# A fused attention and mixture-of-experts kernel: three early blocks of one expert, three of the second, then a fourth of each, in an order that is computed anew

## The chip, the core and the metric

The kernel runs on one core of a Trainium2 chip. Its metric is the device time of one execution in microseconds (us). The engines are PE (TensorE: matmuls, with its weight loads listed apart as PEld), DVE (VectorE), ACT (ScalarE), POOL (GpSimd) and SP (SyncE, which issues most DMAs). Each engine works through a queue of its own in the order in which the program was written, and waits at the head of that queue for whatever the next instruction needs.

## The reference

A causal attention with a sliding window, then a mixture of eight experts of which each row uses two:

```python
B, H, S, D = 8, 8, 576, 64
scores = q @ k.T / sqrt(D) + slopes[h] * -|i - j|      # kept where 0 <= i - j < 128
attn   = exp(scores - max); attn /= attn.sum() + 1e-9
x      = (attn @ v) laid out as 4608 rows x 512
logits = x @ w_gate + log1p(exp(x @ w_noise)) * noise   # 8 experts
top2   = the two largest of each row; weights = softmax over the two
for e in range(8):                                      # w1 512 x 1024, w2 1024 x 512
    out[rows of e] += weight * (relu(x[rows of e] @ w1[e]) @ w2[e])
```

## The kernel before

**The stages.** The attention comes as 32 pairs of heads (8 batches of 4 pairs), and each pair makes nine score blocks along the sequence, 288 in all. For each block PE computes the scores (L518), DVE adds the bias and finds the maxima (L524, two instructions a block), ACT takes the exponentials (L532), PE transposes them (L539), ACT or DVE copies them out of the accumulator bank, and PE multiplies by the values (L553). When a batch is done, `rows` divides by the denominators, writes the rows to memory and computes the gate; `route` then picks the two experts of each row, and gives each its place in the lists of the experts (`slots`).

**The experts.** A matrix is kept as two half-precision parts, high and low, and each product is three matmuls. `weight` loads one eighth (a *step*, 512 KB) of an expert's two matrices into one of 24 tiles `held`, and takes its absolute maxima (`wam`): on ACT as two activations that write into `junk` (L1147), on DVE as one reduction (L1143). When all eight steps of an expert have theirs, `powers_of_weights` makes a power of two from them, and `split` writes the high halves (a copy with a scale, L287 on ACT and L289 on DVE) and the low halves (L1185 on DVE, L1182 and the line behind it on POOL) over the raw weights. `tokens` gathers a block's rows by an indirect DMA (L1218); `fit` scales and splits them (the last part is L1256), and a transposing DMA (L1264) brings them into `ax` or `bx`. `mm1` (L1273) makes a step of the hidden layer; `middle` applies the relu (high part on ACT, L1301, or on DVE; low part always on DVE, L1324, into `ahl` or `bhl`); `mm2` (L1333) multiplies by the second matrix.

**Two waves.** The first wave has eight small blocks, four of each of the first two experts: 256, 256, 256 and 192 rows. The fourth of an expert, say, is written 0.3 for expert 0. The rows of such a block are taken from the lists as they stand after 2, 4, 6 and 7 of the 8 batches (`CUTS`; the ids that belong to them come from L1008), so that the first wave runs while the attention still goes on. `SEQUENCE` is the order of these blocks. The second wave has the rest: one block for each of the first two experts and three for each of the others. Between the waves `overflow` computes on one partition a table of the rows that an expert has beyond its capacity (L1549 to L1574, in the tiles `spared`).

**What sets the order.** No loop order is written out. While the program is built, `Order` plays the whole run through with a duration for each operation. Each step is a strand that yields its operations with a rank, and an engine of the model takes the one with the lowest rank among those that are ready; what is taken is written into the program at that place. A strand that yields an operation of several instructions (a lambda with a list) has them in one piece. `either(...)` offers an operation to ACT and to DVE, each with its own duration and rank offset, and the first to take it keeps it. The numbers at the top of the program are ranks and offsets: `WEIGHTS` and `HOLD` for when an expert's steps are loaded, `GATE` for the rows of a batch, `FFN0` and `FFN1` for the early blocks, `BIG` and `PARTS` for the maxima and the halves of the later experts' weights, `LATE` for the second engine of an `either`. For POOL, the model also blocks DVE for a fixed time beside three of its operations (`slows`).

In the time after, lines 5 to 6 lower in number mean the same operations (L1324 before is L1319 after, L1143 and L1147 are L1141 and L1145).

Of the kernel before, what the change touches and what calls it, by code (L numbers as in the profile page):

```python
# [15 lines left out]
OP = mybir.AluOpType  # L16
AX = mybir.AxisListType
# [5 lines left out]
NQ = 5  # L23
# [19 lines left out]
ZERO = 714.8  # L43
LOAD = 296.4
VALUES = 533.9
GATE = (-2.7, -33.5)
ROUTE = 0
SCATTER = (-245.2, -812.9, 94.5)
FFN0, FFN1 = 207.0, 403.8
WEIGHTS = ((-24.5, 112.1), (505.6, 7.5))  # L50
SEQUENCE = ((0, 0), (0, 1), (1, 0), (1, 1), (0, 2), (1, 2), (0, 3), (1, 3))
TOKENS = -211.8
STAGE = (130.6, -162.3, -306.6, -45.6, -45.9, -85.0, 118.1, -29.9)
MIDDLE = 410.3
RESULT = -460.1
WEIGHTS_LATE = 152.7
SOON = 370.9
LISTED = (-405.9, 168.6)
BIG, PARTS = -57.2, 468.7
TIGHT = (1, 5, 7)  # L60
LATE = (-344.6, -113.3, -185.1, 116.9, -276.1, 92.1, -240.2, -276.5, 251.3, -261.2, 47.5, 142.3, 39.7, 106.3)
# [4 lines left out]
REST = 5.6  # L66
PACE = (8.9, 10.6)
HOLD = (-83.6, 40.7)
AHEAD = -25.9
GATHER_LAG, SCATTER_LAG, LISTED_LAG, TURN_LAG = 4.4, 5.0, 3.0, 4.0  # L70
STAY, TURN = -100.0, 0.13
# [16 lines left out]
class Op:  # L88


    def __init__(self, on, emit, join=True, shape=0, slows=0.0):
        self.slows = slows
        self.on, self.emit, self.join, self.taken = on, emit, join, False
        self.shape, self.leaves = shape if isinstance(shape, tuple) else (shape, shape)
# [16 lines left out]
class Order:  # L111
# [136 lines left out]
def attention_moe(ctx: ExitStack, tc: tile.TileContext, qk_, v, w_gate, w_noise, noise, w12,  # L248
# [410 lines left out]
    def rows(b, t):  # L659
# [5 lines left out]
        def turned():  # L665
            for e in range(2):
                for h in range(2):
                    from_ = (h + e) % 2 * 64
                    nc.vector.tensor_scalar(den[e * 64:e * 64 + 64, 0:NQ - e, h:H:2], dens[b][from_:from_ + 64, e:NS:2], 1e-9, None,
                                            op0=OP.add)  # L670
# [111 lines left out]
    def route(b):  # L782
# [160 lines left out]
        else:  # L943
            yield Op((("POOL", 1.55, rank), ("DVE", 0.8, rank + LATE[10])), lambda g: tables(engine[g], 2), slows=0.4)
# [185 lines left out]
    def weight(e, f, t, rank):  # L1130
# [44 lines left out]
    def split(e, f, z, t, parts, rank, both):  # L1175
# [11 lines left out]
        if e < EARLY:  # L1187
            yield Op((("POOL", 2.85, rank), ("DVE", 0.66, rank + WEIGHTS_LATE)), low, slows=0.6)
# [195 lines left out]
    def last_downs(blk, rank):  # L1384
# [15 lines left out]
        for z, on in enumerate(("ACT", "DVE")):  # L1400
# [138 lines left out]
    def overflow():  # L1539
# [20 lines left out]
        def compare():  # L1560
            V.tensor_tensor(ge[:, 0], jt[:, :, None].to_broadcast(shape), cnt[:, 3:4].to_broadcast(shape), op=OP.is_ge)
            V.tensor_mul(ge[:, 1], ge[:, 0], cnt[:, 1:2].to_broadcast(shape))

        def rows():
            V.tensor_reduce(red, ge, axis=AX.X, op=OP.add)
# [4 lines left out]
            V.tensor_mul(ge[:, 0], ge[:, 0], capv[:, None, :].to_broadcast(shape))  # L1570
            V.tensor_reduce(jt, ge[:, 0], axis=AX.X, op=OP.add)
# [157 lines left out]
```

## Time and profile before

| what | before |
|---|---|
| device time, median of 3 runs | 1053.86 us (1053.57 to 1054.55) |
| the profiled execution | 1055.3 us, span of the trace 1053.5 us |
| mean granted clock of TensorE | 0.993 |
| PE busy | 1014.3 us, 96% of the span |
| DVE busy | 633.3 us, 60% |
| ACT busy | 495.2 us, 47% |
| POOL busy | 346.4 us, 33% |
| DMA, mean over the span | 137 GB/s |

An engine's busy share is a mean over stages that are limited by different things. DVE and ACT are nine tenths busy in the first slices, while the attention runs, and at two to four tenths from the middle on, where PE multiplies by the experts' weights without a break. So the table says which engine is fullest over the whole span, and the stretches have to be looked at one by one. The idle time of PE (the span less 1014.3 us) is 39.2 us.

### The profile page before, as it was taken

The numbers are of one execution on the slowest core, as the hardware profiler recorded it, in microseconds if no ns is written. First come the engines' busy times: TensorE is split into PE (matmuls) and PEld (weight loads), VectorE is DVE, ScalarE is ACT, GpSimd is POOL, SyncE is SP. The second block draws the span as 40 slices with busy tenths as digits, with TensorE's granted clock in tenths as the row PEclk, the third lists the DMA queues.
The fourth block names the chain that finished last, engine by engine and source line by source line (L and its number), as shares of the span: only waits on it lengthen the run. The fifth ranks groups of instructions, "written<-read, shape, count | busy, mean of one in ns | idle before, by whom it ended". The sixth has DMA issues, their size and how long they took to land.

```text
span 1053.5 us, 23716 instructions
## 1 busy us (share of the span) xinstructions
PE 1014.3 (96%) x8942; PEld 639.7 (61%) x8942; DVE 633.3 (60%) x2264; ACT 495.2 (47%) x1402; POOL 346.4 (33%) x458
## 2 busy tenths in 40 slices
PE   7989798999999899999999999999999999999997
PEld 4756666776676579754565457545744664564455
DVE  8998998978787982254559544744494364332111
ACT  8998887766422552231346333632353343332211
POOL 1476963334233431330333232312332320421102
PEclk9999999999999999999999999999999999999999
DMA  9868796635258882385765576519563752653113
GB/s 339 329 233 284 249 305 202 184 96 122 35 108 247 172 105 38 87 190 171 103 144 107 112 151 126 124 40 173 122 135 50 150 82 51 122 68 52 17 24 50
DMA packets 130340, 144.79 MB, mean 137 GB/s; under 512 B 90400, under 2 KB 91504, under 8 KB 130224
## 3 DMA queue, kind: packets, MB, share of 16 engines
q1 hardware_dynamic: 112704, 103.92, 36.1%
q0 software_dynamic: 17520, 39.34, 21.8%
q8 instruction: 71, 1.16, 0.5%
q14 instruction: 45, 0.37, 0.1%
HBM read 82.89 MB, written 40.91 MB: 118 GB/s over the span
## 4 chain that ended last, share of the span: by engine, by line
PE 81%; DVE 12%; ACT 4%; issue 2%; POOL 1%; DMA 0%; DVEq 0%; POOLq 0%; ACTq 0%
PE bank L1273 34%; PE bank L1333 28%; PE bank L1338 6%; PE bank L553 4%; PE bank L518 3%; PE bank L539 3%; DVE p L524 3%; ACT p L532 2%; DVE held L1185 1%; DVE x L704 1%; PE bank L724 1%; ACT pT L287 1%; DVE xt L1256 1%; PE bank L1446 1%; PE bank L701 1%
## 5 line engine op out<-in xcount | busy, mean ns | idle before, releaser
L1273 PEld LDWEIGHTS <-held 128*128 128x128 f16 x2424 | 234.7, 98 | 124.5 <-issue 0.6
L1273 PE MATMUL bank<-bx,held 128*128 128x512 f16 (+7 forms) x1752 | 300.6, 324 | 0.0
L1324 DVE SCALAR_TENSOR_TENSOR bhl<-bank,bhh 128x384 f16<-128x384 f32 (+6 forms) x152 | 84.6, 557 | 281.2 <-ACT bhh L1301 281.0
L1468 POOL DMA_INDIRECT out_dram<-yo,ix x62 | 99.4, 1603 | 426.6 <-ACT yo L287 366.8
L1301 ACT ACTIVATE bhh<-bank 128x512 f16<-128x512 f32 (+6 forms) x134 | 65.4, 488 | 325.9 <-PE bank L1273 317.2
L1333 PE MATMUL bank<-held,bhh 128*128 128x512 f16 x696 | 207.0, 379 | 0.0
L1333 PE MATMUL bank<-held,bhl 128*128 128x512 f16 x348 | 131.9, 379 | 0.0
L532 ACT ACTIVATE p<-p,nm 128x192 f32<-128x192 f32 (+2 forms) x288 | 121.9, 428 | 14.0 <-DVE nm L524 13.6
L1333 PEld LDWEIGHTS <-bhh 128*128 128x128 f16 x768 | 75.2, 98 | 80.7
L1218 POOL DMA_INDIRECT xg<-xs_dram,ix x62 | 69.2, 1116 | 51.9 <-issue 16.6
L524 DVE CUSTOM_DVE_ANT_0 p<-bank,bias 128x192 f32<-128x192 f32 (+2 forms) x288 | 79.6, 328 | 9.5 <-PE bank L518 6.6
L518 PE MATMUL bank<-qk 64*64 64x192 f32 (+2 forms) x1152 | 67.0, 328 | 12.2 <-DVE nm L524 8.5
L1273 PE MATMUL bank<-ax,held 128*128 128x256 f16 (+1 forms) x672 | 77.0, 268 | 0.0
L539 PE MATMUL bank<-ident,p 128*128 128x128 f32 x416 | 67.5, 285 | 9.2 <-ACT pT L287 2.2
L287 ACT ACTIVATE held<-held,wsc 128x512 f16<-128x512 f32 x96 | 65.7, 716 | 17.6 <-DVE held L1185 16.2
L1333 PEld LDWEIGHTS <-bhl 128*128 128x128 f16 x384 | 37.6, 98 | 45.5 <-DVE bhl L1324 0.5
L539 PEld LDWEIGHTS bank<-ident,p 128*128 128x128 f32 x416 | 44.7, 141 | 31.9 <-ACT p L532 10.5
L1143 DVE TENSOR_REDUCE wam<-held 128x2 f32<-128x1024 f32 x53 | 63.7, 1210 | 0.3 <-DMA held<-in_w_dram 0.3
L1185 DVE SCALAR_TENSOR_TENSOR held<-held,wsc,held 128x512 f16<-128x512 f32 x88 | 63.2, 756 | 0.0
L553 PE MATMUL bank<-pT,vraw 64*64 64x64 f32 (+1 forms) x2048 | 61.3, 227 | 0.4 <-DVE x L704 0.3
L553 PEld LDWEIGHTS bank<-pT,vraw 64*64 64x64 f32 (+1 forms) x2048 | 55.1, 138 | 8.8 <-issue 3.5
L287 ACT ACTIVATE xt<-xg,fit 128x512 f16<-128x512 f32 (+5 forms) x60 | 43.0, 718 | 32.6 <-DVE fit L1232 30.9
(254 smaller groups left out, 1499.3 us busy)
## 6 DMA issues: line engine op xcount, KB each, us to landing
held<-in_w_dram SPq DMA_DIRECT2D x60, 512.0 KB
qk<-in_qk_dram SPq DMA_DIRECT2D x31, 576.0 KB
vraw<-in_v_dram SPq DMA_DIRECT2D x16, 640.0 KB
out_dram<-xg SPq DMA_DIRECT2D x10, 1024.0 KB
xs_dram<-x SPq DMA_DIRECT2D x32, 256.0 KB
spare<-in_w_dram SPq DMA_DIRECT2D x4, 512.0 KB
xs_dram<-x SPq DMA_DIRECT2D x8, 128.0 KB
xs_dram<-xg SPq DMA_DIRECT2D x1, 1024.0 KB
```

The costliest lines, as they stand in the source:

```text
L287: nc.scalar.activation(o, i, AF.Copy, **kw)
L518: nc.tensor.matmul(s[j % 2][half:half + 64, o:o + c], qk[rows, j * 64:j * 64 + 64], qk[rows, k1 - c:k1], start=True, stop=True)
L524: nc.vector.tensor_tensor_reduce(out=p[:, place(j):place(j) + c], in0=s[z][:, o:o + c], in1=bias4[:, g, z, 192 - c:192], scale=-0.125, sca ...
L532: nc.scalar.activation(pv, pv, AF.Exp, bias=nm[:, z:z + 1], scale=-1.0, accum_out=den[:, j, g:g + 1])
L539: nc.tensor.transpose(t[:, z * 128:z * 128 + 128], p[:, a * 128:a * 128 + 128], ident)
L553: nc.tensor.matmul(o[half, j // 2 * SUB:j // 2 * SUB + SUB], t[rows, block, hh:hh + D], pt[rows, slot, from_:from_ + 64], start=first_, st ...
L1185: nc.vector.scalar_tensor_tensor(lo, t, sc, hi, op0=OP.mult, op1=OP.subtract)
L1218: yield pool(1.04, rank, lambda: nc.gpsimd.indirect_dma_start(out=xg[0:r], out_offset=None, in_=xs[0:blk.rows], in_offset=bass.IndirectOff ...
L1273: nc.tensor.matmul(t[:, 0:blk.n], wp[:, c], blk.x[:, x + c, 0:blk.n], start=c == 0 and z == 0, stop=c == 3 and z == 2)
L1324: yield dve(0.07 + c * 0.00104, rank - MIDDLE, lambda: nc.vector.scalar_tensor_tensor(hl[:, 0:c], t[:, 0:c], 0.0, hh[:, 0:c], op0=OP.max, ...
L1333: nc.tensor.matmul(blk.y[j][0:r], h[:, cs], wp, start=f == 0 and m == 0, stop=f == 7 and m == 2)
L1468: ins = nc.gpsimd.indirect_dma_start(out=out, out_offset=bass.IndirectOffsetOnAxis(ap=blk.ix[0:r, j:j + 1], axis=0), in_=t[0:r], in_offset ...
```

## The change

All edits are in the program that computes the order and in the steps that it places; the matmuls are the same.

- The early blocks come as 0.0, 0.1, 0.2, 1.0, 1.1, 1.2, 0.3, 1.3, where they alternated from the third on.
- The second expert's eight steps are loaded later, by `WEIGHTS` and `HOLD`.
- The sums of the denominators in `rows` go to POOL (to DVE for the last batch), and the reciprocal becomes an operation of its own on DVE.
- The maxima of all experts' weights may be taken by ACT or DVE, where those of the later six were DVE's alone. The low halves of the third expert may be made on POOL, as those of the first two.
- The table of the overflow is twelve operations in the queue, in place of two that had 2 and 10 instructions.
- The last block's second half of a result is copied by ACT, where DVE did it.
- `slows` goes: the model no longer blocks DVE beside POOL.
- All ranks and offsets have new values, and the order is made anew with them.

```diff
-WEIGHTS = ((-24.5, 112.1), (505.6, 7.5))
-SEQUENCE = ((0, 0), (0, 1), (1, 0), (1, 1), (0, 2), (1, 2), (0, 3), (1, 3))
+WEIGHTS = ((63.8, 81.5), (510.7, 23.6))
+SEQUENCE = ((0, 0), (0, 1), (0, 2), (1, 0), (1, 1), (1, 2), (0, 3), (1, 3))
...
-BIG, PARTS = -57.2, 468.7
+BIG, PARTS = 30.4, 41.2
...
-HOLD = (-83.6, 40.7)
+HOLD = (-77.6, 178.2)
...
-    def __init__(self, on, emit, join=True, shape=0, slows=0.0):
-        self.slows = slows
+    def __init__(self, on, emit, join=True, shape=0):
...
-        elif e == "POOL" and what.slows:
-            self.busy["DVE"] = max(self.busy["DVE"], self.now) + what.slows
-            self.at(self.busy["DVE"], lambda: self.dispatch("DVE"))
...
-        def turned():
+        on = nc.vector if b == B - 1 else nc.gpsimd
+
+        def collected():
             for e in range(2):
                 for h in range(2):
...
-                    nc.vector.tensor_scalar(den[...], dens[b][...], 1e-9, None, op0=OP.add)
-            nc.vector.reciprocal(den, den)
-        yield dve(1.3, rank, turned)
+                    on.tensor_scalar(den[...], dens[b][...], 1e-9, None, op0=OP.add)
+        yield (dve if b == B - 1 else pool)(1.0, rank, collected)
+        yield dve(0.36, rank, lambda: nc.vector.reciprocal(den, den))
...
-        if e < EARLY:
-            yield either(1.35, 1.13, rank, LATE[12], largest)
-        else:
-            yield dve(1.13, rank + BIG, lambda: largest("DVE"))
+        yield either(1.6, 1.13, rank + (BIG if e >= EARLY else 0), LATE[12 if e < EARLY else 14], largest)
...
-        if e < EARLY:
-            yield Op((("POOL", 2.85, rank), ("DVE", 0.66, rank + WEIGHTS_LATE)), low, slows=0.6)
+        if e <= EARLY:
+            yield Op((("POOL", 2.85, rank), ("DVE", 0.66, rank + WEIGHTS_LATE)), low)
...
-        for z, on in enumerate(("ACT", "DVE")):
+        for z, on in enumerate(("ACT", "ACT")):
...
-        yield dve(1.5, 1110, compare)
-        yield dve(2.2, 1120, rows)
+        for z, (us, emit) in enumerate(steps_):      # the same twelve instructions
+            yield dve(us, 1130 + 2 * z, emit)
```

Three places show what this does to the queues. The first is DVE's queue at the overflow's table, while the early blocks run. `spared` are the tiles of the table, `ahl` the low parts of the hidden layer, `wam` the maxima of the third expert's raw weights in `held16` and its followers. Before:

```order
L1568 CAST bias4_135<-spared_5082 1x80
L1569 TENSOR_TENSOR spared_5082<-iota8_142,spared_5082 1x640
L1570 TENSOR_TENSOR spared_5082<-spared_5082,capv_197 1x640
L1571 TENSOR_REDUCE spared_5082<-spared_5082 1x80
L1572 SCALAR_TENSOR_TENSOR spared_5082<-spared_5082 1x80
L1573 SCALAR_TENSOR_TENSOR spared_5082<-spared_5082 1x80
L1574 TENSOR_SCALAR bias4_135<-spared_5082 1x80
L1324 SCALAR_TENSOR_TENSOR ahl1_212<-bank5_71,ahh1_209 128x256
L1143 TENSOR_REDUCE wam_189<-held16_5065 128x2
L1324 SCALAR_TENSOR_TENSOR ahl2_213<-bank0_66,ahh2_210 128x256
L1143 TENSOR_REDUCE wam_189<-held17_5066 128x2
L1143 TENSOR_REDUCE wam_189<-held18_5067 128x2
```

After, from a little earlier in the table on:

```order
L1319 SCALAR_TENSOR_TENSOR ahl2_213<-bank0_66,ahh2_210 128x256
L1559 TENSOR_SCALAR spared_5158<-spared_5158 1x80
L1560 TENSOR_TENSOR spared_5158<-spared_5158 1x80
L1561 CAST bias4_135<-spared_5158 1x80
L1562 TENSOR_TENSOR spared_5158<-iota8_142,spared_5158 1x640
L1319 SCALAR_TENSOR_TENSOR ahl0_211<-bank1_67,ahh0_208 128x256
L1563 TENSOR_TENSOR spared_5158<-spared_5158,capv_197 1x640
L1564 TENSOR_REDUCE spared_5158<-spared_5158 1x80
L1319 SCALAR_TENSOR_TENSOR ahl1_212<-bank5_71,ahh1_209 128x256
L1565 SCALAR_TENSOR_TENSOR spared_5158<-spared_5158 1x80
L1566 SCALAR_TENSOR_TENSOR spared_5158<-spared_5158 1x80
L1567 TENSOR_SCALAR bias4_135<-spared_5158 1x80
```

The operations of the table no longer stand in one row: three of L1319 (L1324 before) stand among them, and no `wam` of the third expert follows.

The second place is SP's queue at the loads of the second expert's eight steps (`held8` to `held15` out of `in_w_dram`). Before, they stand among the first loads of the attention (`qk`, `vraw`, and the noise `noi`), ahead of all rows of the first batch:

```order
L415 DMA noi_141<-in_noise_dram 128x320
L1135 DMA held8_121<-in_w_dram 128x1024
L1135 DMA held9_122<-in_w_dram 128x1024
L1135 DMA held10_123<-in_w_dram 128x1024
L1135 DMA held11_124<-in_w_dram 128x1024
L1135 DMA held12_125<-in_w_dram 128x1024
L471 DMA vraw1_83<-in_v_dram 128x1280
L1135 DMA held13_126<-in_w_dram 128x1024
L457 DMA qk1_79<-in_qk_dram 128x1152
L1135 DMA held14_127<-in_w_dram 128x1024
L1135 DMA held15_128<-in_w_dram 128x1024
L418 DMA slots_dram<-xg2_133 128x352
```

After, they stand between rows of the third batch (`x0` to `x3`, written to `xs_dram`) and the store of a gate (`gd`):

```order
L707 DMA xs_dram<-x3_109 128x512
L1133 DMA held8_121<-in_w_dram 128x1024
L467 DMA vraw0_82<-in_v_dram 128x1280
L1133 DMA held9_122<-in_w_dram 128x1024
L1133 DMA held10_123<-in_w_dram 128x1024
L1133 DMA held11_124<-in_w_dram 128x1024
L1133 DMA held12_125<-in_w_dram 128x1024
L1133 DMA held13_126<-in_w_dram 128x1024
L1133 DMA held14_127<-in_w_dram 128x1024
L1133 DMA held15_128<-in_w_dram 128x1024
L453 DMA qk3_81<-in_qk_dram 128x1152
L976 DMA xs_dram<-gd_178 128x4x8
```

The eight loads have moved by some 75 places in SP's queue; the same instructions, the same sizes.

The third place is ACT's queue where the second wave begins: `ahh` are the high parts of the last early block, `bhh` those of the first block of the second wave. Before:

```order
L1301 ACTIVATE ahh1_209<-bank5_71 128x192
L1301 ACTIVATE ahh2_210<-bank0_66 128x192
L1301 ACTIVATE ahh0_208<-bank1_67 128x192
L287 ACTIVATE yt0_5083<-bank7_73 128x192
L287 ACTIVATE yt1_5084<-bank3_69 128x192
L287 ACTIVATE yt2_5085<-bank6_72 128x192
L287 ACTIVATE yt3_5086<-bank4_70 128x192
L287 ACTIVATE yo1_205<-bank2_68,gw4_202 128x512
L287 ACTIVATE yo2_5073<-bank2_68,gw4_202 64x512
L1301 ACTIVATE bhh1_5060<-bank0_66 128x256
L1301 ACTIVATE bhh2_5061<-bank1_67 128x256
L1301 ACTIVATE bhh0_5059<-bank5_71 128x256
```

After:

```order
L1296 ACTIVATE ahh0_208<-bank1_67 128x192
L1296 ACTIVATE ahh1_209<-bank5_71 128x192
L1296 ACTIVATE ahh2_210<-bank0_66 128x192
L1145 ACTIVATE junk_188,wam_189<-held16_5141 128x512 x2
L1145 ACTIVATE junk_188,wam_189<-held17_5142 128x512 x2
L1145 ACTIVATE junk_188,wam_189<-held18_5143 128x512 x2
L1145 ACTIVATE junk_188,wam_189<-held19_5144 128x512 x2
L1145 ACTIVATE junk_188,wam_189<-held20_5145 128x512 x2
L1145 ACTIVATE junk_188,wam_189<-held21_5146 128x512 x2
L1296 ACTIVATE bhh2_5137<-bank1_67 128x256
L1296 ACTIVATE bhh0_5135<-bank5_71 128x256
L1145 ACTIVATE junk_188,wam_189<-held23_5148 128x512 x2
```

Between the last early block and the second wave's first relus on ACT stand six pairs of maxima of the third expert's weights, and a seventh pair two relus later; before there were results of an early block (`yt`, `yo`) and no maxima.

More of the change, by code (lines that the diff above doesn't have):

```diff
@@ L42 @@
 LISTS = ((0, EARLY, DONE[-1], (CAP - DONE[-1] + 127) // 128), (EARLY, E, 0, (CAP + 127) // 128))
[L43 to L46, printed above, removed]
+ZERO = 781.9
+LOAD = 234.3
+VALUES = 544.1
+GATE = (-40.1, -141.2)
 ROUTE = 0
-SCATTER = (-245.2, -812.9, 94.5)
-FFN0, FFN1 = 207.0, 403.8
-WEIGHTS = ((-24.5, 112.1), (505.6, 7.5))
-SEQUENCE = ((0, 0), (0, 1), (1, 0), (1, 1), (0, 2), (1, 2), (0, 3), (1, 3))
[L52 to L58, printed above, removed]
-BIG, PARTS = -57.2, 468.7
+SCATTER = (15.2, -920.1, 412.5)
+FFN0, FFN1 = 185.5, 400.5
+WEIGHTS = ((63.8, 81.5), (510.7, 23.6))
+SEQUENCE = ((0, 0), (0, 1), (0, 2), (1, 0), (1, 1), (1, 2), (0, 3), (1, 3))
+TOKENS = -212.1
+STAGE = (310.1, -61.0, -339.5, -54.3, 18.9, -292.4, 181.0, 131.1)
+MIDDLE = 85.6
+RESULT = -852.8
+WEIGHTS_LATE = 159.2
+SOON = 274.1
+LISTED = (-393.8, 515.9)
+BIG, PARTS = 30.4, 41.2
 TIGHT = (1, 5, 7)
-LATE = (-344.6, -113.3, -185.1, 116.9, -276.1, 92.1, -240.2, -276.5, 251.3, -261.2, 47.5, 142.3, 39.7, 106.3)
+LATE = (-46.9, 63.5, -185.4, 171.9, -556.1, 6.2, -257.4, -114.3, 214.1, -84.7, 99.5, 263.1, 212.5, 74.3, 64.7)
 LAG = 0.2
@@ L65 @@
 DMA_LAG = 4.0
-REST = 5.6
-PACE = (8.9, 10.6)
-HOLD = (-83.6, 40.7)
-AHEAD = -25.9
+REST = 84.1
+PACE = (-25.0, -151.2)
+HOLD = (-77.6, 178.2)
+AHEAD = -92.9
 GATHER_LAG, SCATTER_LAG, LISTED_LAG, TURN_LAG = 4.4, 5.0, 3.0, 4.0
-STAY, TURN = -100.0, 0.13
+STAY, TURN = 32.5, 0.13
 TICK, WARM = 3.413, 1.28
@@ L668, in turned @@
                     from_ = (h + e) % 2 * 64
-                    nc.vector.tensor_scalar(den[e * 64:e * 64 + 64, 0:NQ - e, h:H:2], dens[b][from_:from_ + 64, e:NS:2], 1e-9, None,
-                                            op0=OP.add)
-            nc.vector.reciprocal(den, den)
-        yield dve(1.3, rank, turned)
+                    on.tensor_scalar(den[e * 64:e * 64 + 64, 0:NQ - e, h:H:2], dens[b][from_:from_ + 64, e:NS:2], 1e-9, None,
+                                     op0=OP.add)
+        yield (dve if b == B - 1 else pool)(1.0, rank, collected)
+        yield dve(0.36, rank, lambda: nc.vector.reciprocal(den, den))
         put(denr, dens[b])
@@ L943, in route @@
         else:
-            yield Op((("POOL", 1.55, rank), ("DVE", 0.8, rank + LATE[10])), lambda g: tables(engine[g], 2), slows=0.4)
+            yield Op((("POOL", 1.55, rank), ("DVE", 0.8, rank + LATE[10])), lambda g: tables(engine[g], 2))
         a = yield (tb, rank)
```

28 lines of the change are left out of this document (14 added, 14 removed).

## The prediction

> **What bounds the kernel now.** I read first where TensorE (PE) stands idle, stretch by stretch, then who releases it, then the chain through the worst place. The borders of the stretches are the 36th, the 216th and the last (288th) score block of the attention. Columns: us; busy us and count of PE, PEld, DVE, ACT, POOL; granted clock; DMA share; GB/s.
>
> ```profile
> 0.00:28.80 28.80, 21.20 (x329) 14.46 (x331) 23.59 (x107) 23.53 (x90) 3.22 (x24) 0.95 0.91 346
> 28.80:183.20 154.40, 138.86 (x2440) 101.78 (x2436) 138.87 (x642) 134.24 (x515) 98.54 (x123) 0.99 0.78 264
> 183.20:269.40 86.20, 84.30 (x1245) 61.66 (x1247) 73.43 (x379) 57.05 (x223) 32.12 (x68) 1.00 0.53 133
> 269.40:325.00 55.60, 54.57 (x574) 39.07 (x571) 40.65 (x177) 18.12 (x51) 19.14 (x31) 1.00 0.41 86
> 325.00:400.00 75.00, 69.74 (x510) 47.59 (x508) 63.10 (x189) 34.90 (x75) 23.49 (x26) 0.98 0.86 171
> 400.00:1035.00 635.00, 635.00 (x3792) 367.50 (x3790) 292.74 (x777) 225.81 (x449) 166.69 (x181) 1.00 0.52 101
> 1035.00:1053.50 18.50, 10.63 (x75) 7.58 (x72) 0.89 (x2) 1.53 (x3) 3.21 (x5) 0.91 0.22 30
> ```
>
> PE is the bound: from 400 to 1035 it has no gap. The order holds the same matmuls after the change, so only PE's idle time can go: 7.6 us at the start, 15.5 and 1.9 in the attention, 1.0, then 5.3 between 325 and 400 while the first wave of expert blocks runs, and 7.9 at the end. In the second stretch three engines are almost equally full (PE 138.86, DVE 138.87, ACT 134.24 of 154.40). The score blocks place the borders: the row of DVE's L524 alone (two instructions for each block; one on a border counts twice).
>
> ```profile
> 28.80:183.20 154.40, 49.79 (x361) 0.99 0.78 264
> 183.20:269.40 86.20, 20.29 (x147) 1.00 0.53 133
> ```
>
> Who ends PE's waits over the whole span, and the two long gaps of the fifth stretch with their releasers:
>
> ```profile
> PE bank L518 <- DVE nm L524: 8.5, 14, 1.6
> PE bank L539 <- ACT pT L287: 2.2, 5, 0.9
> PE bank L736 <- ACT pT L287: 1.1, 2, 0.8
> 332.78 0.39 PE L1333 MATMUL bank<-held,ahl 128*128 128x512 f16 x1 [1.90 <-DVE ahl L1324]
> 346.42 0.39 PE L1333 MATMUL bank<-spare,ahl 128*128 128x512 f16 x1 [2.20 <-DVE fit L492]
> ```
>
> The chain through that stretch (start, us, what) tells what DVE did instead of the awaited L1324, and the clock in the ten microseconds around the second gap:
>
> ```profile
> 327.35 1.39 DVE spared L1565
> ...
> 329.98 0.82 DVE spared L1570
> ...
> 332.20 0.19 DVE bias L1574
> 332.39 0.34 DVE ahl L1324
> ...
> 341.53 4.51 DVE wam L1143 x4
> 340.00:350.00 10.00, 7.80 (x46) 4.83 (x45) 8.91 (x25) 4.73 (x13) 6.40 (x8) 0.84 0.81 159
> ```
>
> From 327.35 to 332.39 DVE runs the overflow's table, 5.0 us in one piece; from 341.53 it runs four maxima of the third expert's weights, 4.51 us in one piece. Each time the low part of the hidden layer stands behind them, and PE behind that.
>
> **The change, part by part.**
>
> *A, the stretch 325 to 400.* The overflow's steps are queued one by one, and in the new order three L1324 stand between its two halves and its end. The eight maxima of the third expert leave this place: they stand behind the last block of the first wave, seven of eight on ACT, and its 16 halvings (hi and lo) behind them. DVE's rows for both here:
>
> ```profile
> L1143 DVE TENSOR_REDUCE wam<-held 128x2 f32<-128x1024 f32 x8 | 9.3, 1206 | 0.0
> L1185 DVE SCALAR_TENSOR_TENSOR held<-held,wsc,held 128x512 f16<-128x512 f32 x16 | 11.4, 741 | 0.0
> ```
>
> That is 9.3 + 11.4 = 20.7 of DVE's 63.10 us; 42 of 75 us remain, so DVE no longer decides there. What goes: the gaps of 1.90 and 2.20 us, and the slow clock, 0.16 x 10 = 1.6 us. Sum -5.7 us. Ends: -6.9 (all 5.3 us of idle and the clock) and 0 (a new wait takes the place). Late next is nothing that I find: the longest DVE piece left there is the first half of the overflow, nine small operations like L1574 (0.19), two like L1570 (0.82) and L1565's sum (1.39), together some 4.7 us, but it stands behind two L1324 in a row, so PE has two steps in hand where it had one.
> [...] The trace shows half rate for about 3.2 us (0.16 x 10 / 0.5) after a gap of only 2.20 us, with PE busy 7.80 of 10. [...]
>
> *B, the attention, 28.8 to 269.4.* In SP's queue the second expert's eight loads stand between the gates that the third and the fourth batch store, where before they stood ahead of the first batch's rows; their preparation moves with them from the second stretch to the third. Rows of the second stretch:
>
> ```profile
> L287 ACT ACTIVATE held<-held,wsc 128x512 f16<-128x512 f32 x23 | 16.2, 716 | 0.0
> L1147 ACT ACTIVATE junk<-held 128x512 bf16<-128x512 f32 x10 | 6.3, 630 | 0.2
> L1147 ACT ACTIVATION_READ_ACCUMULATOR junk<-held 128x1 f32 x10 | 1.9, 194 | 0.0
> L669 DVE TENSOR_SCALAR byrow<-den 64x20 f32<-64x20 f32 (+1 forms) x20 | 4.8, 238 | 0.2
> L1143 DVE TENSOR_REDUCE wam<-held 128x2 f32<-128x1024 f32 x4 | 4.8, 1213 | 0.0
> ```
>
> Counted in the two orders between the same score blocks: ACT has 16 fewer halvings (16 x 0.716 = 11.5) and 8 fewer maxima (8 x (0.630 + 0.194) = 6.6): 18 us less, 134 to 116. DVE loses 20 sums of the denominators, now on POOL (4.8), and two maxima (2.4), and gains evacuations that ACT gave up and two tokens' halves: together +2, 139 to 141. PE gets the first expert's block 21 score blocks earlier and more of the attention's own matmuls: +7, 139 to 146. In the third stretch DVE gains 15 halvings (8 x 0.741 and 7 shorter ones) and 3 maxima and loses tokens' work: +6, 73 to 79; ACT +7, 57 to 64; PE -5, 84 to 80. So ACT falls out of the contest in the second stretch, and DVE draws level with PE in the third. What counts is PE's idle time in both, 15.5 + 1.9 = 17.4 us. Ends: if the three-engine coupling was the cause, half of it goes, -8; if DVE keeps in the third stretch the share of idle that it has in the second (154.40 / 138.87 = 1.11), 79 becomes 88 where the stretch took 86, and PE's longer order in the second costs 4: +6. I take the half of the waits that ACT ended (2.2 + 1.1): -1.6, since the evacuations go to DVE, which ends the larger waits (8.5 us).
>
> *C, the third block.* The blocks now come as 0.0, 0.1, 0.2 of the first expert; the third needs the ids of cut 2, which come after batch 5. In the order PE has 2.5 us less work ahead of the third block than before, where it began at 293.61: with B it gets there at about 290. Ids, gather and transposes before:
>
> ```profile
> 280.07 0.16 DVE L1008 SCALAR_TENSOR_TENSOR ids<-bank,ids 128x4 int32<-128x4 f32 x1
> 291.58 1.04 POOL L1218 DMA_INDIRECT xg<-xs_dram,cl  x1 [0.30 <-issue]
> 304.61 2.65 SPq L1264 DMA_TRANSPOSE ax<-xt  x2
> 255.38 1.06 POOL L1218 DMA_INDIRECT xg<-xs_dram,cl  x1 [0.15 <-issue]
> 264.69 7.06 SPq L1264 DMA_TRANSPOSE ax<-xt  x2
> 293.61 1.15 PE L1273 MATMUL bank<-ax,held 128*128 128x256 f16 x9
> ```
>
> The ids of cut 2 came 97 us after the 216th score block (280.1 - 183.2). In DVE's queue the same amount of work stands between the two (83 us against 83), so 83 to 97 us after, at 267 to 280; from the gather to the transposes went 9.3 and 13.0 us; the transposes take 3 to 7. Ready at 280 to 300 against 290: from 0 to +10. Most of that lies under zero, since DVE has fewer gaps there than before: +1.5.
>
> *D, the start of the second wave.* ACT gets six pairs of maxima in a row: 6 x 2 x (0.630 + 0.194) = 9.9 us, with the first relu that ACT has to do in the new wave, that of its third step, behind them. What PE can do meanwhile, by the chain's rows for 192 columns and 256 (24 matmuls each; 512 columns are taken as twice 256):
>
> ```profile
> 410.12 1.98 PE bank L1273 x24
> 335.27 2.62 PE bank L1273 x24
> ```
>
> In the order stand 24 matmuls of 192 columns, 54 of 256 and 12 of 512 until that relu's result is read: 1.98 + 5.9 + 2.6 = 10.5 us against 9.9 (the relus of the first two steps are on DVE). Ends 0 and +3, if ACT starts late; I take +0.5.
>
> *At nothing:* the later experts' maxima, half on ACT now, and the earlier loads lie beside 635 us of full PE, with DVE at 293 and ACT at 226 us: cover enough. If that cover failed it would be seen as PE gaps after 420. The last half copy goes from DVE to ACT; both engines have been idle for microseconds there: 0.
>
> *Sum:* -5.7 - 1.6 + 1.5 + 0.5 = -5.3. The profiled execution took 1055.3 us (span 1053.5); it would take 1050.0. The median of the runs is 1.4 below the profiled one, 1053.86, so 1048.6.
>
> **The rivals.**
> *R1, ACT was what coupled the attention.* For it: second stretch, no engine above 90% and yet 15.5 us of idle PE. Against: the larger waits name DVE. B is then -8, C and D 0: 1053.86 - 5.7 - 8 = 1040; in the middle 1042.
> *R2, the third block's tokens are late.* For it: with the 97 us of before and 13 + 7 after, they land at 300. Then PE stands for up to 10 us at its first matmul, and 1.6 us of slow clock follow. Typical +6.6 in place of 1.5: 1053.7; at the far end 1060.
> *R3, slower: DVE is held by POOL in the third stretch.* Eight pairs of the second expert's low halves run on POOL there, beside DVE's own two-input halvings.
>
> ```profile
> L1185 DVE SCALAR_TENSOR_TENSOR held<-held,wsc,held 128x512 f16<-128x512 f32 x8 | 7.5, 936 | 0.0
> L1182 POOL TENSOR_SCALAR held<-held,wsc 128x512 f32<-128x512 f32 x24 | 39.4, 1640 | 42.2 <-DVE spare L289 36.8 <-ACT held L287 5.3
> ```
>
> In the stretch with POOL's halvings, L1185 took 936 ns, without them 741: 0.2 us each, 2 us for eight. If each of the eight held DVE for a whole 1.64 us, DVE's 79 became 92, 6 more than the stretch took, and B turned to about +8: 1058. It decides from 8 us of lost DVE time on; the two rows speak for 2.
> [...]
> *R4, the relief is taken back.* DVE's 20.7 us move to steps 65 to 80, where D or a late halving may stop PE as before: A is 0 in sum: 1054.
>
> **How the numbers follow.** A difference of 0.2% (2.1 us) is about what a measurement of this kernel can tell from none. The forecast's case 0.45, its own range 1045 to 1051.7; R1 0.18; R2 0.17 (0.02 faster, 0.07 same, 0.08 slower); R3 0.06; R4 0.14 (0.02, 0.09, 0.03). Faster 0.45 + 0.18 + 0.02 + 0.02 = 0.67; same 0.16; slower 0.08 + 0.06 + 0.03 = 0.17. The range reaches from the end of R1, 1040, to 1057, which leaves out R3 and the far end of R2 and R1, some 0.15.
>
> **What would show it.** A: no PE gap over 1 us between 325 and 400, clock 1.00 there. B: PE idle in the attention 14 to 17 us, ACT at about 116 us of the second stretch. C: the first matmul of the third block within 2 us of the one before it. D: no PE gap at the first blocks of the second wave. Wrong it would be if PE waits for DVE's L524 more than 8.5 us, or for transposes, or if the time after 420 holds gaps.

## The result, and the profile after

| what | before | after |
|---|---|---|
| device time, median of 4 runs each | 1054.2 us | 1066.45 us (1064.25 to 1067.39) |
| ratio to before, 95% interval | | 1.0102 (1.0087 to 1.0118) |
| the profiled execution, its span | 1055.3, 1053.5 us | 1067.39, 1065.2 us |

The changed kernel is 11 to 12 us slower (1.02% of 1054 are 10.8 us), where 5 us less was forecast. All times below are compared as ratios to runs of the kernel before beside them, since that kernel itself took 1052 to 1055.6 us in the different comparisons, and one profiled execution can stand up to 3.6 us from its median; 0.1% is 1.05 us.

The stretches of the changed kernel, with the same columns as in the prediction; the borders are again the 36th, the 216th and the last score block, which now come at 29.6, 187.0 and 284.1 us, and the second wave begins at 429.0 (420.8 before):

```profile
0.00:29.60 29.60, 22.27 (x376) 15.73 (x376) 23.70 (x105) 23.88 (x92) 3.24 (x24) 1.00 0.92 343
29.60:187.00 157.40, 139.80 (x2472) 103.54 (x2470) 135.99 (x664) 118.27 (x474) 65.86 (x125) 0.99 0.75 244
187.00:284.10 97.10, 86.40 (x1177) 61.73 (x1176) 87.95 (x368) 65.86 (x237) 54.26 (x85) 0.98 0.48 134
284.10:325.00 40.90, 39.05 (x446) 27.56 (x444) 27.70 (x109) 13.49 (x39) 13.51 (x19) 1.00 0.48 106
325.00:400.00 75.00, 72.97 (x520) 48.51 (x518) 50.61 (x190) 28.12 (x69) 27.36 (x32) 1.00 0.75 171
400.00:429.00 29.00, 29.00 (x352) 28.96 (x351) 8.92 (x31) 10.82 (x32) 4.60 (x6) 1.00 0.39 57
429.00:500.00 71.00, 68.79 (x424) 40.60 (x423) 42.25 (x109) 28.10 (x64) 32.19 (x29) 1.00 0.69 191
```

PE's idle time in them, stretch less busy: 7.3, 17.6, 10.7, 1.9, 2.0, 0 and 2.2 us. The third row is where the time went: 10.7 us of idle PE where there were 1.9. DVE is busy 87.95 of 97.10 us there; before it was 73.43 of 86.20. The last row shows a loss that the kernel before does not have at all, since PE had no gap from 400 to 1035. The fifth shows the gain that was forecast: 2.0 where there were 5.3, and the clock at 1.00.

Who ends PE's waits in the third stretch (us in all, times, the longest):

```profile
PE bank L851 <- DVE hot L847: 1.8, 1, 1.8
PE bank L535 <- ACT pT L283: 1.4, 4, 0.5
PE bank L535 <- ACT held L283: 1.1, 1, 1.1
PE bank L549 <- DVE pT L287: 1.0, 1, 1.0
PE bank L734 <- DVE x L702: 1.0, 1, 1.0
PE bank L990 <- DVE x L702: 1.0, 1, 1.0
```

No single wait stands out: PE waits once or twice for each of many DVE steps, which is what a late engine looks like. DVE's and POOL's groups there (busy, mean ns of one | idle before):

```profile
L1180 DVE SCALAR_TENSOR_TENSOR held<-held,wsc,held 128x512 f16<-128x512 f32 x8 | 7.9, 996 | 0.0
L839 DVE TENSOR_TENSOR hot<-ef,steps 128x800 f16<-128x800 f32 x3 | 3.9, 1307 | 0.0
L825 DVE TENSOR_SCALAR lines<-lines 128x8 int32<-128x8 int32 x3 | 2.2, 724 | 0.1
L847 DVE TENSOR_TENSOR hot<-hot,numbers 128x640 f16<-128x640 f16 x1 | 1.4, 1437 | 0.0
L966 DVE TENSOR_SCALAR cl<-ids 128x4 int32<-128x4 int32 x1 | 0.8, 825 | 0.0
L1177 POOL TENSOR_SCALAR held<-held,wsc 128x512 f32<-128x512 f32 x8 | 14.9, 1860 | 0.4 <-POOL byrow L667 0.4
L1178 POOL TENSOR_TENSOR held<-held,held 128x512 f16<-128x512 f32 x8 | 9.6, 1205 | 0.7
```

The same steps in the third stretch of the kernel before, where POOL has no halvings:

```profile
L841 DVE TENSOR_TENSOR hot<-ef,steps 128x800 f16<-128x800 f32 x3 | 3.0, 985 | 0.0
L849 DVE TENSOR_TENSOR hot<-hot,numbers 128x640 f16<-128x640 f16 x1 | 0.8, 807 | 0.0
L827 DVE TENSOR_SCALAR lines<-lines 128x8 int32<-128x8 int32 x4 | 0.7, 172 | 0.1
```

Instructions of the same shape last up to four times as long, by the means of their groups. To size this I took for each DVE instruction what it lasted beyond the lower quartile of its like (same operation and operands, both traces) and added up what is over 40 ns; below this is called the *hold*. In the third stretch of the changed kernel it is 10.0 us in 20 instructions, all of them beside a POOL instruction, 7.0 us of it beside the halvings L1177 and L1178. Less the hold DVE has 78 us of work, as counted ahead (79).

### The profile page after: what moved, and what is told of

Same layout as the page of the kernel before. It is cut to its first block, busy times and chain, and to the rows that moved or that the text cites. A ratio compares the mean times of both kernels' runs of the same rounds, so it can differ in the third digit from the quotient of the medians.

```text
span 1065.2 us, 23866 instructions
## 1 busy us (share of the span) xinstructions
PE 1015.6 (95%) x8942; PEld 640.1 (60%) x8942; DVE 618.1 (58%) x2258; ACT 521.0 (49%) x1500; POOL 358.7 (34%) x480
## 4 chain that ended last, share of the span: by engine, by line
PE 78%; DVE 14%; DMA 2%; issue 2%; ACT 1%; POOL 1%; SPq 0%; DVEq 0%; POOLq 0%; ACTq 0%
PE bank L1268 34%; PE bank L1328 28%; PE bank L1333 6%; PE bank L549 4%; DVE p L520 3%; PE bank L514 2%; DVE held L1180 2%; PE bank L535 2%; DVE x L702 1%; DMA held<-in_w_dram 1%; DVE held L285 1%; DMA vraw<-in_v_dram 1%; DVE pT L287 1%; ACT p L528 1%; PE bank L699 1%
## 5 line engine op out<-in xcount | busy, mean ns | idle before, releaser
L1463 POOL DMA_INDIRECT out_dram<-yo,ix x62 | 108.9, 1757 | 376.8 <-ACT yo L283 349.8
L1319 DVE SCALAR_TENSOR_TENSOR bhl<-bank,bhh 128x384 f16<-128x384 f32 (+6 forms) x152 | 84.5, 556 | 249.6 <-ACT bhh L1296 244.1
L1296 ACT ACTIVATE bhh<-bank 128x512 f16<-128x512 f32 (+6 forms) x127 | 63.0, 497 | 287.9 <-PE bank L1268 280.6
L1180 DVE SCALAR_TENSOR_TENSOR held<-held,wsc,held 128x512 f16<-128x512 f32 x89 | 68.2, 811 | 0.0
L514 PEld LDWEIGHTS bank<-qk 64*64 64x64 f32 x1152 | 40.8, 137 | 30.3 <-DVE nm L520 19.9
L1251 DVE SCALAR_TENSOR_TENSOR xt<-xg,fit,xt 128x512 f16<-128x512 f32 (+1 forms) x78 | 57.3, 750 | 2.8 <-ACT xt L283 2.3
L283 ACT ACTIVATE xt<-xg,fit 128x512 f16<-128x512 f32 (+5 forms) x54 | 38.6, 718 | 41.1 <-DVE fit L1227 36.1
```

What stands on the lines that cost most here:

```text
L514: nc.tensor.matmul(s[j % 2][half:half + 64, o:o + c], qk[rows, j * 64:j * 64 + 64], qk[rows, k1 - c:k1], start=True, stop=True)
L1180: nc.vector.scalar_tensor_tensor(lo, t, sc, hi, op0=OP.mult, op1=OP.subtract)
L1319: yield dve(0.07 + c * 0.00104, rank - MIDDLE, lambda: nc.vector.scalar_tensor_tensor(hl[:, 0:c], t[:, 0:c], 0.0, hh[:, 0:c], op0=OP.max, ...
L1463: ins = nc.gpsimd.indirect_dma_start(out=out, out_offset=bass.IndirectOffsetOnAxis(ap=blk.ix[0:r, j:j + 1], axis=0), in_=t[0:r], in_offset ...
```

## The experiments

Ratios are to the kernel before, with 95% intervals. Where a part is cut, the change to the code says so.

**Is it POOL's halving of the second expert?** Three kernels with the changed kernel's order, all of whose other instructions stand as they stood; the first two leave the eight low halves out:

```diff
         def low(g):
+            if g == "POOL" and e == 1:          # low1_brief
+                nc.gpsimd.memset(lo, 0.0)
+                return
...
+                for _ in range(5):              # low1_fill, ahead of that memset
+                    nc.gpsimd.memset(t, 0.0)
...
-            if g == "POOL":
+            if g == "POOL" and e != 1:          # low1_on_dve
```

> The changed kernel in its own order, but each of POOL's eight low halves of the second expert (a multiply and a subtraction) is one short fill of the low part, so that part of the result is wrong. H (DVE is held by POOL: in the stretch from the 216th to the last score block, 187 to 284 us, 20 of DVE's instructions lasted 10.0 us longer than their like, 7.0 of it beside these halvings, and DVE is what fills the stretch, 88.0 of 97.1 us): the stretch falls by 7 to 8, DVE busy there by 7, time 1066.4 - 7.5 = 1059. Q (POOL's queue is too long: 24.5 us of halvings delay the routing's POOL steps, for which DVE and PE then wait): also faster, 1056 to 1062; the next run tells it from H. L (the stretch is long because the second expert's other work on DVE has moved into it): 1064 to 1067.

> As the run before, but POOL fills in place of each of the eight low halves: five times the raw half and once the low part, about as long as the halving, and it reads nothing; that part of the result is wrong. H (an instruction of POOL that reads holds DVE): as the run before, 1059, and DVE's excess in the stretch under 4 us. Q (POOL's queue): as the changed kernel, 1065 to 1067. If any POOL instruction holds DVE: 1065 to 1067 too, but with DVE's excess still at 7 to 10 us.

> The changed kernel in its own order, with the eight low halves of the second expert that POOL made written into DVE's queue at the same places. H: 7.0 us of hold go, 8 x 0.74 = 5.9 us of work come: DVE's 88 becomes 87, time 1064 to 1067. Q: POOL's queue is free, DVE has 5.9 more: 1062 to 1068. L (DVE's own work fills the stretch, nothing is held): 88 + 5.9, times 1.1, 1072.

Measured: low1_brief 1.0049 (1.0032 to 1.0066), low1_fill 1.0082 (1.0065 to 1.0099), low1_on_dve 1.0085 (1.0068 to 1.0101). The third stretch of the three, in this order, each from its own profile:

```profile
185.80:276.60 90.80, 84.09 (x1178) 60.39 (x1176) 82.00 (x368) 65.28 (x237) 34.20 (x77) 1.00 0.52 142
```

```profile
186.30:281.20 94.90, 85.39 (x1178) 62.06 (x1177) 82.53 (x369) 65.23 (x237) 54.70 (x117) 0.98 0.49 134
```

```profile
186.00:280.60 94.60, 85.94 (x1178) 61.26 (x1177) 85.80 (x376) 65.91 (x237) 31.76 (x69) 0.98 0.47 134
```

With the halves cut short the stretch falls by 6.3 us and the whole by 0.53%, 5.6 us: L is out. The fills keep POOL as busy as before (54.70 against 54.26), free DVE as much (82.53), and yet give only 2.1 us: here neither H nor Q alone, and with intervals of 0.2% each the split was open. With the eight on DVE the kernel is at 1063 by its ratio, inside Q's range and 1 us under H's; L's 1072 is out again.

**The hold, instruction by instruction.** From the order of time in the changed kernel (start, us, engine):

```profile
216.92 1.15 POOL L1178 TENSOR_TENSOR held<-held,held 128x512 f16<-128x512 f32 x1
217.02 1.33 DVE L285 TENSOR_SCALAR held<-held,wsc 128x512 f16<-128x512 f32 x1
...
219.87 1.16 POOL L1178 TENSOR_TENSOR held<-held,held 128x512 f16<-128x512 f32 x1
...
220.23 0.82 DVE L966 TENSOR_SCALAR cl<-ids 128x4 int32<-128x4 int32 x1
```

and, in low1_brief, the same L966 and behind it another L285 of the same shape:

```profile
216.72 0.16 DVE L966 TENSOR_SCALAR cl<-ids 128x4 int32<-128x4 int32 x1
216.79 0.48 DVE L285 TENSOR_SCALAR held<-held,wsc 128x512 f16<-128x512 f32 x1
```

L966 has four elements a partition and needs 0.16 us; beside POOL's subtraction it ends at 221.05, when that has ended (221.03). By these ends it stood until POOL was done, rather than ran slower. In the kernel before, six small steps that are held beside the same subtraction (L1183 there) end 21 to 56 ns behind it.

**The second expert's halves on DVE as well.** One more kernel (halves1_brief), again in the order of the changed kernel, leaves out all halves of the second expert that DVE (15) or POOL (8) made; short fills stand in their places. If DVE's work set the stretch, it was expected to fall to 86 or 87 us and the ratio to 1.001; if not, 89 to 91 us and 1.004 to 1.005. Measured: 1.0027 (1.0017 to 1.0038), and the third stretch:

```profile
187.10:275.10 88.00, 83.62 (x1177) 60.47 (x1176) 76.84 (x368) 64.75 (x237) 32.33 (x77) 1.00 0.53 147
```

That lies between the two. PE's idle time in the stretch is 10.7 us in the changed kernel, 6.7 without POOL's eight halves, 4.4 without DVE's too, and 1.9 in the kernel before. So the second expert's halves bring 6.3 of the 8.8 us that were added there, 4.0 of them by way of POOL.

**Is it the place of the second expert's work, the sequence, or the model?** Three orders made anew, with one thing each put back (`slows` stood beside two kinds of operation on POOL, the low halves and a routing table, with 0.6 and 0.4 us):

```diff
-WEIGHTS = ((63.8, 81.5), (510.7, 23.6));  HOLD = (-77.6, 178.2)
+WEIGHTS = ((63.8, 81.5), (505.6, 7.5));   HOLD = (-77.6, 40.7)       # after_early1
...
+SEQUENCE = ((0, 0), (0, 1), (1, 0), (1, 1), (0, 2), (1, 2), (0, 3), (1, 3))   # after_oldseq
...
+            self.busy["DVE"] = max(self.busy["DVE"], self.now) + what.slows      # after_slows, with 0.6 and 0.4
```

> The changed kernel with the two numbers for the load of the second expert's weights as they were before (early), all else as changed; the order is made anew from there. M (half of the loss in the stretch from the 216th to the last score block is the second expert's own work there, half is the hold by POOL; both go back into the stretch before): PE's idle time in that stretch falls from 10.7 to 2 to 4 us, the stretch before gains 2 to 5 us of idle; 4 to 7 us less than the changed kernel, ratio to before 1.003 to 1.006. Rival (the stretch is long for another reason, the three early blocks in a row or the new ranks): ratio 1.010.

> The changed kernel with the early blocks in the order of before (the experts alternate from the third block on), all else as changed; DVE's queue is the same up to the 216th score block. If three blocks of one expert in a row crowd the third stretch (the third block's tokens and ids are made there, at 223 to 245 us): 3 to 5 us less than the changed kernel, ratio to before 1.005 to 1.007. If the sequence costs nothing by itself: 1.009 to 1.012.

> The changed kernel with the old rule in the order's model (DVE is blocked for 0.6 us beside each low half on POOL and 0.4 us beside a routing table on POOL), all else as changed; the order is made anew from 30 us on. If the loss is that the order no longer reckons with the hold: POOL gets fewer halves or DVE's steps stand elsewhere, 4 to 8 us less than the changed kernel, ratio to before 1.003 to 1.006. If the new numbers themselves make the order worse: 1.008 or more.

Measured: 1.0108 (1.009 to 1.0126), 1.0115 (1.0098 to 1.0132), 1.0159 (1.0142 to 1.0176). None gains anything. In after_early1 the two stretches of the attention read:

```profile
29.30:195.20 165.90, 145.47 (x2478) 106.65 (x2476) 151.72 (x692) 129.04 (x506) 97.14 (x143) 0.95 0.77 252
195.20:299.40 104.20, 98.59 (x1342) 71.78 (x1338) 70.09 (x361) 61.65 (x230) 37.26 (x80) 0.98 0.46 114
```

The third stretch is relieved, though less than M said (5.6 us idle where M had 2 to 4; 0.2 us of hold), but the second has 20.4 us of idle, 8.7 us of hold, and a clock of 0.95, by estimate another 8 us ((1 - 0.95) x 165.9). The loss moved with the work, and the whole is what the rival had said, 1.010; of the rival's two causes after_oldseq rules out the sequence, and the new ranks were not tested by themselves.

**Code or numbers?** The code of before with all new numbers, and the reverse:

```diff
-ZERO = 714.8            # old_code_new_numbers: all numbers down to STAY, TURN as in the changed kernel
+ZERO = 781.9
...
-ZERO = 781.9            # new_code_old_numbers: as before, and LATE[14] = 64.7
+ZERO = 714.8
...
```

> The code of before with all new numbers at the top (ranks, offsets and the sequence of early blocks); the order is made anew. If the numbers make the loss: ratio to before 1.008 or more. If the edits of the code make it: 1.003 or less.

> The changed code with the numbers of before (and 64.7 for the one new offset); the order is made anew. If the edits of the code make the loss: ratio to before 1.008 or more. If the numbers make it: 1.003 or less. Numbers and code belong together, and both crossed kernels may be slow for that: then this pair does not tell them apart.

Measured: 1.0173 (1.0156 to 1.019) and 1.0155 (1.0132 to 1.0178). Both crossings are slower than either kernel, so, as the expectation allowed, they do not tell code from numbers.

**All of POOL's low halves, in both kernels.** Again in each kernel's own order; `brief` is one fill in place of each halving, `fill` five of them:

```diff
             if g == "POOL":
-                nc.gpsimd.tensor_scalar(t, t, sc, None, op0=OP.mult)
-                nc.gpsimd.tensor_sub(lo, t, hi)
+                for _ in range(4):              # fill only
+                    nc.gpsimd.memset(t, 0.0)
+                nc.gpsimd.memset(lo, 0.0)
```

> The kernel before in its own order, with each of POOL's 24 low halves of the first two experts one short fill, so that part of the result is wrong. There too DVE was held, by 11 us in the stretch from 29 to 183 us. If that hold costs as much a microsecond as in the changed kernel (6.3 us of the stretch for 7.0): 8 to 10 us less, ratio 0.991. If it was mostly hidden there, since PE, DVE and ACT are about equally full: 0 to 3 us less, ratio 0.997 to 1.000.

> The changed kernel in its own order, with all 21 low halves on POOL (nine of the first expert, eight of the second, four of the third) one short fill each, so that part of the result is wrong. To be set beside the same cut in the kernel before (ratio 0.9945, which freed DVE of 11 us). If the hold makes the difference between the two kernels: ratio to before 0.995 to 0.998, the gap between the two cut kernels under 0.3%. If the order makes it, and both pay the hold alike: 1.002 to 1.005 (0.5 to 0.8% for 21.8 us of hold and less), the gap between the cut kernels 0.8 to 1.0%.

> The changed kernel in its own order, with POOL filling in place of each of its 21 low halves: four times the raw half and once the low part, 5 x 0.56 = 2.8 us for the 2.7 to 3.1 us of a halving, and it reads nothing; that part of the result is wrong. If the halves cost by holding DVE (15.5 us of excess beside them): close to the run with all of them cut short, ratio to before 0.998 to 1.001. If they cost by making POOL's queue late: close to the changed kernel, 1.006 to 1.010. In the run with the second expert's fills about two fifths of the relief came from the hold: by that 1.005.

> The same in the kernel before, for its 24 low halves. If they cost by holding DVE: near the run with all of them cut short, 0.995 to 0.997. If by POOL's queue: 0.999 to 1.001.

| ratio to before | as it is | fills | cut short |
|---|---|---|---|
| before, 24 halvings | 1 | 0.9965 (0.9952 to 0.9977) | 0.9945 (0.9929 to 0.9962) |
| after, 21 halvings | 1.0102 (1.0087 to 1.0118) | 1.0004 (0.9995 to 1.0012) | 0.9971 (0.9962 to 0.9981) |

The busy line of the page of the changed kernel with fills:

```profile
PE 1011.9 (96%) x8942; PEld 640.8 (61%) x8942; DVE 605.4 (58%) x2258; ACT 520.4 (49%) x1500; POOL 354.0 (34%) x543
```

POOL is as busy as in the changed kernel (354.0 against 358.7 us), DVE does the same instructions in 605.4 us where it took 618.1, and the time falls by 0.98%. So about three quarters of what the halvings cost there (0.98 of 1.31%) goes with what a halving does to DVE and a fill of the same total length does not; for the second expert's eight alone it was two fifths, 0.20 of 0.53%, with some 0.24% of uncertainty on each. The rest is POOL's queue and the holds that fills still make. Fills differ in two ways: they read nothing, and each is shorter (0.56 us against 1.86 and 1.2). Of DVE's own low halves (L1180), which read two tiles, 10 of 20 are held beside POOL's halvings in the changed kernel, by 5.8 us in all, and beside the fills none of 22; that the reading makes this and not the length is my inference. For the high halves (L285) it is open: 8 of 14 are held beside halvings, by 4.2 us, and 8 of 15 beside fills, by 2.2.

By these ratios the halvings cost 13.8 us in the changed kernel and 5.8 before; the 5.8 lie between the two expectations for before_low_brief. Cut short in both, 0.26% is left between the two kernels (0.9971 / 0.9945); by the two intervals added as squares, 0.2% uncertain. So some 8 of the 10.8 us by which they differ are the halvings, though there are three fewer of them; by the four intervals this 8 is uncertain by 2.6, and by the fills it is 6.6.

PE's idle time in the attention does not go the same way. The two stretches without the halvings, first the two kernels with short fills (before, after), then the two with fills as long:

```profile
29.60:174.70 145.10, 134.69 (x2392) 98.99 (x2388) 129.88 (x644) 132.51 (x515) 40.23 (x95) 1.00 0.83 281
174.70:260.10 85.40, 83.91 (x1243) 61.69 (x1245) 73.19 (x377) 56.93 (x223) 32.16 (x68) 1.00 0.53 135
30.30:182.50 152.20, 137.89 (x2473) 102.27 (x2470) 131.41 (x666) 118.34 (x475) 43.75 (x114) 1.00 0.78 253
182.50:274.80 92.30, 85.54 (x1178) 61.88 (x1177) 82.27 (x368) 65.47 (x237) 34.23 (x77) 0.98 0.52 138
```

```profile
29.40:177.10 147.70, 135.18 (x2394) 99.07 (x2390) 132.40 (x644) 133.41 (x516) 91.69 (x195) 1.00 0.81 276
177.10:262.50 85.40, 83.96 (x1244) 61.70 (x1246) 73.19 (x379) 57.01 (x223) 32.15 (x68) 1.00 0.52 134
29.60:184.40 154.80, 139.07 (x2475) 103.39 (x2470) 132.91 (x664) 118.40 (x476) 64.61 (x152) 0.99 0.77 250
184.40:276.60 92.20, 85.18 (x1178) 61.44 (x1177) 81.95 (x368) 65.33 (x237) 51.67 (x109) 0.98 0.49 138
```

PE is idle there for 17.4 us in the kernel before and 28.3 in the changed one; without the halvings for 11.9 and 21.1, with fills as long for 14.0 and 22.8. The halvings cost idle time in the attention of both kernels, 5.5 and 7.2 us, and some 9 of the 10.9 us between the kernels stay when they are gone. In the whole these 9 us are partly made up between the last score block and the second wave, where PE's idle time is 5.9 us before and 2.3 after in the pair with fills; the spans of that pair, 1045.8 and 1051.6, are 5.8 us apart. The other place where the halvings tell is the second wave, which the next run takes up. In PE's idle time the two places show some 2 and 2 to 3 of the 8 us; where the rest lies is not shown.

**The second wave's share.** Four of the third expert's low halves are on POOL in the changed kernel:

```diff
-            if g == "POOL":
+            if g == "POOL" and e != EARLY:      # low2_on_dve
```

> The changed kernel in its own order, with the four low halves of the third expert that POOL made (in the second wave, 429 to 500 us) written into DVE's queue at the same places. H: DVE's excess of 5.1 us there goes, 4 x 0.74 = 3.0 us come, and PE's idle of 2.2 us between 450 and 475 (two waits for L1319's and L1298's relus) goes: 1064. Rival (that idle comes from the halves and maxima standing ahead of the relus in DVE's queue, however fast they are): 1066 to 1067.

Measured: 1.0092 (1.0076 to 1.0109), 1.0 us less than the changed kernel, which the intervals do not separate from none. Its profile from the second wave's start on:

```profile
425.30:496.30 71.00, 70.09 (x432) 41.57 (x430) 40.86 (x114) 28.44 (x64) 19.64 (x21) 1.00 0.69 191
```

PE's idle time is 0.9 where it was 2.2; the hold there falls from 5.1 to 0.4 us. The direction is H's, the size about half of it.

**Does ACT's load set the second stretch?**

```diff
+            if 1 <= b <= 5:                     # behind each copy of xu: 512 or 128 columns
+                nc.scalar.activation(junk[:, 0:w], bias4.rearrange("p a b c -> p (a b c)")[:, 0:w], AF.Copy)
```

> The changed kernel in its own order, with 40 extra copies on ACT, 20 of 512 and 20 of 128 columns, spread evenly over the stretch from the 36th to the 216th score block: about 17 us, which ACT lost there by the change. If DVE's chain alone sets that stretch: under 2 us more, ratio to before 1.010 to 1.012. If ACT's load couples it (R1): half or all of the 8 us that R1 gave, ratio 1.014 to 1.018.

Measured: 1.0135 (1.0118 to 1.0152), 3.5 us more for 12 us of busy time put on ACT in that stretch (118.27 to 130.69). The value lies between the two expectations, with an uncertainty of 0.24% on the difference: ACT's load seems to cost something there, and nothing speaks for the 8 us of R1.

**The sums on POOL.**

```diff
-        on = nc.vector if b == B - 1 else nc.gpsimd
+        on = nc.vector
```

> The changed kernel in its own order, with the sums of the denominators written into DVE's queue where the reciprocal stands. DVE gets 28 x 0.22 = 6.1 us and loses the 3.3 us for which it waited for POOL's sums: if DVE sets the pace, 2.8 us more, ratio to before 1.012 to 1.014. If the waits for POOL stand at worse places than the work: 1.006 to 1.009.

Measured: 1.0109 (1.0092 to 1.0125): no difference from the changed kernel. The sums do not matter on either engine.

**Term A by itself, on the kernel before.** The table in twelve operations, then also `either` for all maxima; the orders differ from that of before only from 320 us on:

```diff
-        yield dve(1.5, 1110, compare)
-        yield dve(2.2, 1120, rows)
+        for z, (us, emit) in enumerate(steps_):
+            yield dve(us, 1130 + 2 * z, emit)
...
-            yield dve(1.13, rank + BIG, lambda: largest("DVE"))
+            yield either(1.35, 1.13, rank + BIG, 64.7, largest)      # before_split_wam only
```

> The kernel before, with the overflow's table in twelve operations and nothing else of the change; the order differs from that of before only from the table on (327 us). A holds: the gap of 1.90 us at 331 goes, the four maxima in a row at 341 stay; 1.5 to 2 us less than before, ratio 0.998. Rival (the table's pieces stop another step): ratio 1.000 to 1.002.

> The kernel before, with the table in twelve operations and the maxima of the later experts' weights offered to ACT as well as to DVE; the order differs only from 320 us on. A holds: both gaps (1.90 and 2.20 us) and the 1.6 us of slow clock go, 5.7 us less than before, ratio 0.9946. R4 (the relief is taken back at the start of the second wave): ratio 0.999 to 1.001.

Measured: 1.0008 (0.9996 to 1.0021) and 1.0021 (1.0005 to 1.0037). PE's longest wait between 325 and 400 us in the first:

```profile
PE bank L1273 <- DMA ax<-xt: 2.1, 1, 2.1
```

and in the second:

```profile
PE bank L1273 <- DMA ax<-xt: 3.8, 1, 3.8
PE bank L1333 <- DVE ahh L1303: 1.8, 1, 1.8
```

Both gaps of before are gone, and PE waits instead for the transposed tokens of the next early block. R4's outcome, by another wait than R4 named.

## Why the prediction was wrong, point by point

- **The step that failed** is B, the attention: PE's idle time there was to fall by 1.6 us, and it rose from 17.4 to 28.3, by 10.9. Two things in it were wrong: the price of POOL's halvings for DVE, and the choice of ACT's waits as the measure of what goes.
- **The price of POOL's halvings**, which R3 had at 2 us, was taken from one row of one victim: L1185 took 936 ns with POOL's halvings beside it and 741 without, 0.2 us each, 2 us for eight. But beside POOL many other steps of DVE are held too: the routing's small ones, the high halves, the tokens. Added over all of them the trace of before already held 11.0 us in the second stretch, in 24 instructions. The eight pairs that moved brought 7.0 us, and other POOL work 3.0, to a stretch in which the count had put DVE level with PE (79 us against 80). R3 named the place and the point from which it decides, 8 us of lost DVE time; 10.0 were lost. It had 6 chances in 100. Leaving the eight out takes 5.6 us off the time; leaving out all halvings takes away some 8 of the 10.8 us between the two kernels.
- Of R3's mechanism the rows show more than the prediction had, which named DVE's two-input halvings alone: beside POOL's subtraction (L1178) L285, a copy with a scale, went from 0.48 us to 1.33, and L966, with four elements a partition, from 0.16 to 0.82. Beside POOL's multiplication L817 was held too, but not to the end: at 233.78 it lasted 0.62 us, where its median is 0.17, and ended 0.87 us ahead of the L1177 beside it.
- **ACT's waits as the measure.** B had -1.6 with an upper end of +6. The counts of instructions were right (DVE 78 without the hold); the rule that half of the waits ended by ACT would go was not borne out: ACT has 16 us less in the second stretch (134.24 to 118.27), and PE's idle time there is 17.6 where it was 15.5. Why it rose while PE's work, DVE's and ACT's hardly grew or fell is not settled, and POOL's halvings are not the reason: without them it is 14.3 where it was 10.4. In the third stretch B's own upper end came, in which DVE sets the pace: the stretch took 1.10 times DVE's busy time (97.1 / 87.95), and 1.10 to 1.15 times in the low1 runs, where B had reckoned with 1.11; the hold made 88 us of the 79. So with the halvings out of both kernels B would still have been at +9, and that part is shown as far as the second expert's halves on DVE go (2.3 us) and is open beyond.
- **A** held in the changed kernel: idle from 5.3 to 2.0, the clock to 1.00 from 0.98, 3.3 + 1.5 (0.02 x 75) = 4.8 of the 5.7 us between 325 and 400. The half rate that the prediction speaks of is in the trace of before: a granted clock of 0.50 in each of the three microseconds from 347 to 350. That nothing is late next was true only of that order; in the order of before the transposes were.
- **C** was +1.5: PE's idle time from the last score block to 325 us is 1.9 where it was 1.0, no long wait is for tokens there. Right.
- **D** was +0.5, by ACT at the very start of the second wave: from 400 to 429 PE has no gap. Right. But *at nothing* failed: DVE came late to the relus at 450 to 465, and PE lost 2.2 us, in spite of DVE's many idle stretches later. Of these 1.3 go when POOL's four halvings of the third expert are moved to DVE.
- **R1**'s gain did not come, nor did **R2**, **R4** came where only A's edits were made.

What stays open: most of the 9 us of PE's idle time in the attention that the changed kernel has more even without POOL's halves, the 0.26% between the two kernels that is left of it in the whole, and whether numbers or code make it.

## What to carry to other kernels

Price an engine that disturbs another by all its victims: take each instruction's duration less that of its like when undisturbed, and add up over the stretch; a single group's mean hides it. Such a price has no fixed size: 24 halvings cost 5.8 us in the one order, and 21 cost 13.8 in the other; which neighbours make the difference is not shown. And a large disturbance is not yet the whole reason: leave it out of both kernels, and see whether the idle time between them goes too. And an edit that removes a wait is worth what the next wait leaves of it, so look up when the next operand lands before counting the gain.

## What the runs showed of the hardware

In the changed kernel DVE's L966, with four elements a partition, took 0.82 us beside POOL's L1178 and ended 0.02 us behind it; in low1_brief it took 0.16. Beside POOL's multiplication L817 did not wait for the end: at 233.78 it started 0.09 us behind an L1177 of 1.57 us, lasted 0.62 and ended 0.87 us ahead of it. Of DVE's low halves, which read two tiles, 10 of the 20 that ran beside POOL's halvings in the changed kernel were held, and none of the 22 beside the fills of after_low_fill. Other instructions of DVE were held beside those fills, if less (8 of 15 of L285, by 2.2 us): of the 22.0 us of hold in the changed kernel 11.0 remained with all halvings replaced by fills as long, 4.4 of it beside the fills. Also measured: a stretch in which no PE wait was longer than 1.9 us (after_early1, 29 to 195 us) had a mean granted clock of 0.95, by estimate 8 us (0.05 x 165.9) beside its 20.4 us of idle time.
